# One block of float32 products per chunk, regrouped tiles in halves, and regrouping issued in three parts

## The chip, the core and the metric

The kernel runs on one core of a Trainium2 chip. Its engines are TensorE (PE; its weight loads stand apart as PEld), VectorE (DVE), ScalarE (ACT), GpSimd (POOL) and SyncE (SP), which here issues the DMAs. The metric is the device time of one execution in microseconds, the median of several runs.

## The reference

Three stages follow each other. Cut to what is computed:

```python
X = np.fft.rfft(x, axis=1)                       # x: 8 x 3072 x 256
Y = soft_threshold(X @ (w_r + i w_i) + b, 0.01)  # real and imaginary part apart
x = np.fft.irfft(Y, n=3072, axis=1).reshape(24576, 256)
h = x @ moe_w_in                                 # 256 -> 2048
x = (h - np.tanh(h)) @ moe_w_out                 # 2048 -> 256
logits = x @ phi                                 # 32 slots
d = softmax(logits, axis=0);  slot_in = d.T @ x
slot_out = experts(slot_in)                      # 8 experts, 4 slots each, relu between w1 and w2
out = softmax(logits, axis=1) @ slot_out
```

## The kernel before

The Fourier stage writes its result to DRAM; the token stage reads it back in 48 chunks of 512 tokens; the expert stage runs last. What the change touches is the token stage, and its loop over chunks is most of the time.

A chunk c is loaded transposed as y (128 x 1024). The product with `moe_w_in` is made by a seven-product scheme on 2 x 2 blocks: `wino(c, w, n)`, called P, is six TensorE instructions of 128 x 256 in float32r (a value split into a high and a low part), for one of four column groups w and one of seven products n. A call with n = 1, 4, 6 or 7 is followed by a ScalarE copy of its PSUM bank (line 797). The calls 1, 6, 7 and 4 of one w add to the same bank, so each waits until the copy before it has read the bank. `add` (A, line 804, VectorE) adds a second bank; `gate` (G, line 808, ScalarE) applies tanh. There are eight g tiles per chunk, p = 0 to 7, and six PSUM banks in rotation for P.

The g tiles are used three times, each with plain float32 products of 32 output columns, four of which (a = 0 to 3) lie side by side in the array:

- L, `logit_mm(c, p)`, line 927: the logits, for two g tiles a call, p = 0, 2, 4, 6; the last call adds the four products of line 935 on the raw y tile `yr`.
- DY, `dy_mm(c)`, line 846, and D, `dg_mm(c)`, line 1057: the slot sums, softmax weights `et` times the g values. They want tokens on the partitions. So VectorE transposes each g tile in 32 x 32 blocks (T, `turn_g`, line 878; `turn_yr`, TD, line 867) into two staging tiles, gt0 (g tiles 0 to 3 and yr) and gt1 (4 to 7), with one buffer each, and 32 DMAs per chunk put the blocks into place (`regroup`, "reg", line 894): 16 of 160 KB from gt0, 16 of 128 KB from gt1. Their targets are the four `gq` tiles of a chunk, 9 KB per partition each, out of a ring of five. D makes 16 instructions of 128 x 512 from them; each counts as two in the profile, as every float32 product does.
- `accum_y` and `accum` (accy, acc) then add the PSUM results to running sums.

The order of all engines inside a chunk is written out by hand in the tuple `PLAN`: an entry is a step, its chunk relative to the current one (-1 the one before) and its arguments. Each engine runs its instructions in that order. Before, L of the last three g pairs, ("L", -1, 2) to ("L", -1, 6), stands early in the pass of the next chunk; ("L", 0, 0), ("DY", -1), ("D", -1) stand near the end of the pass.

All DMAs of the token stage are issued by SP, in program order. They share eight semaphores in turn, so a DMA isn't issued before the one eight places earlier has landed. Per chunk SP issues y, yr, the store of the combine weights (line 1041), then reg(-1, 1), then reg(0, 0). In the last chunk the entries ("W", ...) issue expert weights between them.

Of the kernel before, what the change touches and what calls it, by code (L numbers as in the profile page):

```python
# [28 lines left out]
PLAN = (  # L29
# [10 lines left out]
)  # L40
# [608 lines left out]
def token_phase(tc, nch, yd, wh, wl, wp, wy, ident, ew):  # L649
# [9 lines left out]
    with ExitStack() as ctx:  # L659
# [80 lines left out]

        homes = chain(["g5"] + [f"g{k}" for k in range(5)], cycle([f"g{k}" for k in range(5)] + [f"x{k}" for k in range(4)]))

        def g_tile(c, p):
            k = next(homes)
            g = gs[c, p] = (ew.gtp if k == "g5" else ew.gp if k[0] == "g" else ew.txp).tile(
                [128, 2, 512], F32, tag=k, name="g", bufs=1
            )
            return g
# [86 lines left out]
        def dy_mm(c):  # L835


            beside = c < nch - 1
            o = dy[c] = lp[c + 1][:, 256:320] if beside else bank()[:, 0:64]
            if beside:  # L840
                y = [g[:, 0:256].rearrange("p (k f) -> p k f", k=4) for g in gq[c]]
            else:
                y = [yq[c][:, a] for a in range(4)]
            for k in range(4):
                for a in (3, 2, 1, 0):
                    nc.tensor.matmul(
                        o[32 * a:32 * a + 32], ex[c][:, k, :], y[a][:, k], start=k == 0 and not beside, stop=k == 3,
                        skip_group_check=True,
                    )
# [35 lines left out]

        def regroup(c, h):

            t = gt.pop((c, h))
            if h == 0:
                gq[c] = [ew.gq_tile([128, 2304]) for _ in range(4)]  # L890
            for a in range(4):
                o = gq[c][a][:, 1280 * h:1280 + 1024 * h]
                for q in range(4):
                    nc.sync.dma_start(out=o[32 * q:32 * q + 32], in_=t[32 * a:32 * a + 32, q])  # L894

# [74 lines left out]
        def soft_max(c):  # L970
            o = lr[c]
            m = sp.tile([64, 1], F32, tag="m", name="m", bufs=1)
            m2 = sp.tile([32, 1], F32, tag="m2", name="m2", bufs=1)
# [71 lines left out]
        def dg_mm(c):  # L1045

            o = dp[c] = ps2.tile([128, 512], F32, tag="d", name="pd")
            if c < nch - 1:
                parts = [(
                    slice(0, 512), [g[:, 256:2304].rearrange("p (h k f) -> p k h f", h=2, k=4) for g in gq.pop(c)],  # L1050
                )]
            else:
                parts = [(slice(256 * h, 256 * h + 256), [gl[h][:, :, a] for a in range(4)]) for h in range(2)]
# [40 lines left out]
        def chunk(c):  # L1094

            for name, d, *args in PLAN:
# [8 lines left out]
                elif k > 0 and k < nch or k == 0 and name not in "PAG":  # L1105
                    if k < nch - 1 or name not in ("T", "TD", "reg"):
                        if c < nch - 1 or name not in ("D", "DY", "accy"):
                            do(name, k, *args)

        def weights(w):  # L1110

            if w == 0:
                ew.load(12, "y")
                ew.load_ct(0, 16)
            elif w == 1:
                do("reg", nch - 2, 1)
                ew.load_m()
# [12 lines left out]
        for s in range(8):  # L1130
# [30 lines left out]
            if s == 6:  # L1161
                sum_w(1, nc.vector, ((ew.txp, "x2"), (ew.txp, "x3")))
                split_sw(1)
                do("TD", c)
                do("reg", c, 0)
                sum_w(2, nc.vector, ((ew.txp, "x0"), (ew.txp, "x1")))
                sum_w(3, nc.gpsimd, ((ew.txp, "x2"), (ew.gqp, "gq4")))
            yield
# [62 lines left out]
class ExpertWeights:  # L1231
# [6 lines left out]
    def __init__(self, tc, ctx, nch, w1, w2, w_out, md, ctd):  # L1238
# [5 lines left out]
        self.cts = {}  # L1244
        self.turn = 0
        self.spare = {}
# [15 lines left out]
    def open_late(self):  # L1262

        self.tyq = self.pool("tx2", 1)
        pool = self.pool("tc", 1, side="right")
        pool.tile([128, 48], F32, name="pad")
        self.acc = pool.tile([128, 512], F32, name="acc")
# [12 lines left out]

    def gq_tile(self, shape, dtype=F32, k=None):
        if k is None:
            k = self.turn
            self.turn += 1
        return self.gqp.tile(shape, dtype, tag=f"gq{k % 5}", name="gq")

    def load_wo(self):
        w = self.w_out.rearrange("(p F) m -> p F m", F=16)
        self.wo = []
        self.wt = [self.gq_tile([128, 8, 256]) for _ in range(2)]  # L1290
        for k in range(4):
            u = self.wt[k // 2][:, 4 * (k % 2):4 * (k % 2) + 4]
            self.tc.nc.sync.dma_start(out=u, in_=w[:, 4 * k:4 * k + 4])
            self.wo.append(u)

    def load_ct(self, c0, c1):
        n = c1 - c0
        u = self.gtp.tile([128, n, 128], F32, tag="gt1", name="ect", bufs=1) if c0 else self.gq_tile([128, n, 128])
        for c in range(c0, c1, 16):
            m = min(c + 16, c1)  # L1300
            self.tc.nc.sync.dma_start(out=u[:, c - c0:m - c0], in_=self.ctd[:, c:m])
        for c in range(c0, c1, 8):
            self.cts[c] = u[:, c - c0:c - c0 + 8]

# [4 lines left out]
    def pieces(self, j, home):  # L1309
# [18 lines left out]
        if home == "gq":  # L1328
            t = self.gq_tile([128, 2048])
            return [t[:, 512 * i:512 * i + 512] for i in range(4)]  # L1330
        return [u for i in range(2) for u in tile(self.txp, f"x{(2 * j + i) % 4}")]
# [17 lines left out]
def expert_phase(tc, nch, ew, ident, out):  # L1349

    nc = tc.nc
    with ExitStack() as ctx:
# [71 lines left out]
        for i in range(0, nch, 2):  # L1424
# [84 lines left out]
```

## Time and profile before

| | us |
|---|---|
| median of three runs (2195.88 to 2200.4) | 2196.58 |
| the profiled execution, its own time | 2199.71 |
| its span in the trace | 2197.9 |
| PE busy (96% of the span) | 2113.1 |
| DVE busy (83%) | 1825.5 |
| ACT busy (63%) | 1392.0 |
| POOL busy (29%) | 637.3 |

The trace is one execution. An engine's busy time is the union of its instructions; matmul ends are modelled. A wait is put down to what released it. "x32" merges neighbours with the same line. The time from the start of one D (line 1057) to that of the next is the time of a chunk.

### The profile page before, as it was taken

To read this page: it belongs to the slowest core of one execution; us is meant where nothing else is said; L and a number is where in the kernel's file an instruction comes from. 1 tells how busy PE (TensorE), PEld (TensorE's weight loads), DVE (VectorE), ACT (ScalarE), POOL (GpSimd) and SP (SyncE) were. 2 spreads that over 40 slices of the span, in tenths; PEclk is the share of its full clock that TensorE was granted. 3 is DMA by queue.
4 is the path that set the end of the run, shared out by engine and by line. 5 is a ranking of instruction groups with operands and counts; after the bars stand their busy time and mean duration, and the time that the engine had idled before them with its cause. 6 is when DMAs were issued, how large, how long until landed. Compare 5 with 4: busy or idle time off the path is not lost.

```text
span 2197.9 us, 50700 instructions
## 1 busy us (share of the span) xinstructions
PE 2113.1 (96%) x19546; PEld 1755.6 (80%) x19546; DVE 1825.5 (83%) x3650; ACT 1392.0 (63%) x2309; POOL 637.3 (29%) x655
## 2 busy tenths in 40 slices
PE   7999999999999999999999999999999999999976
PEld 3678888888888888888888888888888888888743
DVE  4999989988995888888888888888888888888634
ACT  3466666666655666666676676666667676666623
POOL 1433334434442422222222222222222222222100
PEclk8999999999999999999999999999999999999995
DMA  9678888889666888888888888888888888888899
GB/s 287 207 228 263 249 264 279 249 252 281 193 199 193 200 213 200 206 201 199 202 202 202 205 207 212 200 209 196 196 205 203 199 203 211 202 209 203 239 366 391
DMA packets 251951, 495.76 MB, mean 226 GB/s; under 512 B 36160, under 2 KB 144960, under 8 KB 251328
## 3 DMA queue, kind: packets, MB, share of 16 engines
q1 hardware_dynamic: 251600, 492.49, 82.8%
q8 instruction: 155, 2.54, 0.5%
q14 instruction: 84, 0.69, 0.1%
q10 hardware_dynamic: 112, 0.04, 0.0%
HBM read 164.45 MB, written 106.17 MB: 123 GB/s over the span
## 4 chain that ended last, share of the span: by engine, by line
PE 68%; DMA 14%; SPq 11%; DVE 4%; issue 2%; ACT 1%; POOL 0%; ACTq 0%; POOLq 0%; DVEq 0%
PE ph L786 25%; SPq L894 10%; PE pd L1057 8%; DMA yr<-yd 6%; PE pmix L321 6%; PE pl L927 5%; PE pf L247 5%; PE pi L406 5%; PE pf L280 3%; DMA gq<-gt 3%; PE pi L378 3%; PE pa L321 3%; DMA ewt<-in_moe_w 1%; PE ph L757 1%; DMA out_dram<-ot 1%
## 5 line engine op out<-in xcount | busy, mean ns | idle before, releaser
L797 ACT ACTIVATE g<-ph 128x512 f32<-128x512 f32 x752 | 440.4, 592 | 347.4 <-PE ph L786 326.8
L878 DVE STREAM_TRANSPOSE gt<-g 128x512 f32<-128x512 f32 x752 | 482.4, 684 | 39.5 <-ACT g L808 32.5
L786 PE MATMUL ph<-th,s 128*128 128x256 f32 x2256 | 477.3, 284 | 5.5 <-ACT g L797 4.5
L804 DVE TENSOR_TENSOR g<-ph,g 128x512 f32<-128x512 f32 x564 | 366.4, 676 | 128.8 <-PE ph L786 96.4
L786 PEld LDWEIGHTS ph<-th,s 128*128 128x128 f32 x2256 | 378.1, 190 | 25.5 <-issue 18.9
L808 ACT ACTIVATE g<-g 128x1024 f32<-128x1024 f32 x376 | 390.3, 1052 | 1.8 <-DVE g L804 0.3
L786 PE MATMUL ph<-tl,s 128*128 128x256 f32 x1128 | 318.4, 282 | 0.0
L786 PE MATMUL ph<-yh,wl 128*128 128x256 f32 x1128 | 316.3, 280 | 0.0
L786 PE MATMUL ph<-y,wh 128*128 128x256 f32 x1128 | 315.9, 280 | 0.0
L786 PE MATMUL ph<-yh,wh 128*128 128x256 f32 x1128 | 315.4, 280 | 0.0
L699 POOL TENSOR_TENSOR tl<-tr,th 128x512 fp32r<-128x512 f32 x94 | 121.5, 1293 | 595.9 <-ACT th L698 590.6
L371 POOL TENSOR_TENSOR sw<-t,c 64x256 f32<-64x256 f32 x192 | 169.5, 883 | 157.0 <-DVE c L363 131.7
L786 PEld LDWEIGHTS ph<-tl,s 128*128 128x128 f32 x1128 | 214.0, 190 | 0.0
L786 PEld LDWEIGHTS ph<-yh,wh 128*128 128x128 f32 x1128 | 213.6, 189 | 0.0
L786 PEld LDWEIGHTS ph<-y,wh 128*128 128x128 f32 x1128 | 212.7, 189 | 0.0
L786 PEld LDWEIGHTS ph<-yh,wl 128*128 128x128 f32 x1128 | 212.5, 188 | 0.0
L1057 PE MATMUL pd<-gq,et 128*32 128x512 f32 x1504 | 181.8, 593 | 17.8 <-DMA gq<-gt 16.6
L927 PE MATMUL pl<-g,wp 128*32 128x256 f32 x3072 | 185.9, 382 | 0.0
L693 POOL TENSOR_TENSOR tr<-y 128x256 f32<-128x256 f32 x92 | 68.1, 740 | 401.5 <-DMA y<-yd 401.5
L406 PEld LDWEIGHTS pi<-i,v 96*128 96x128 f32 x1024 | 127.5, 191 | 26.2 <-issue 20.8
L1057 PEld LDWEIGHTS pd<-gq,et 128*32 128x32 f32 x1504 | 86.6, 109 | 75.6 <-issue 22.6
L247 PE MATMUL pf<-xt,c 96*96 96x512 f32 x256 | 134.1, 618 | 11.4 <-DMA xt<-in_x 6.6
(217 smaller groups left out, 4387.3 us busy)
## 6 DMA issues: line engine op xcount, KB each, us to landing
gq<-gt SPq DMA_DIRECT2D x752, 160.0 KB, 3.4
gq<-gt SPq DMA_DIRECT2D x752, 128.0 KB, 3.5
xt<-in_x SPq DMA_DIRECT2D x64, 384.0 KB, 5.3
vd<-vs SPq DMA_DIRECT2D x96, 256.0 KB, 3.2
v<-vd SPq DMA_DIRECT2D x64, 384.0 KB, 5.2
yd<-yt SPq DMA_DIRECT2D x48, 512.0 KB, 5.5
y<-yd SPq DMA_DIRECT2D x48, 512.0 KB, 5.2
yr<-yd SPq DMA_DIRECT2D x48, 512.0 KB, 7.0
```

The costliest lines, as they stand in the source:

```text
L247: nc.tensor.matmul(p[:96], c1, x[:, s], start=True, stop=True)
L321: nc.tensor.matmul(o, st[u], w[m], start=first and k == 0, stop=last and k == 2)
L371: eng.tensor_tensor(out=v[64 * ri:64 * ri + 64, gg], in0=t[q, e], in1=c[q, e], op=ALU.subtract)
L406: nc.tensor.matmul(p[:, a, :], t[:, 4 * u + a, :], i2[:, 96 * n2:96 * n2 + 128], start=True, stop=True)
L786: nc.tensor.matmul(o[:, 256 * j:256 * j + 256], a[u][:, 128 * j:128 * j + 128], y[v], start=new and j == 0 and k == 0, stop=n in (2, 3, 4) ...
L797: nc.scalar.activation(e[n], o.rearrange("p (j n) -> p j n", j=2), AF.Copy)
L804: nc.vector.tensor_tensor(out=h, in0=o, in1=h, op=ALU.add)
L808: nc.scalar.activation(g, g, AF.Tanh)
L878: nc.vector.transpose(out=t[:, :, :, 2 * (p % 4) + u, :], in_=g[:, u, :].rearrange("p (q k i) -> p q k i", q=4, k=4))
L894: nc.sync.dma_start(out=o[32 * q:32 * q + 32], in_=t[32 * a:32 * a + 32, q])
L927: nc.tensor.matmul(lp[c][q:q + 32, 0:256], wp[:, 2 * p + f, :], half_of(c, gs[c, p + f // 2][:, f % 2], h), start=p == 0 and f < 2, stop=F ...
L1057: nc.tensor.matmul(o[32 * a:32 * a + 32, f], ex[c][:, k, :], g[a][:, k], start=k == 0, stop=k == 3)
```

## The change

The entries of `PLAN` are put in another order. In it ("L", -1, 0), ("DY", -2), ("L", -1, 2), ("D", -2), ("L", -1, 4) and ("L", -1, 6) follow each other: the slot sums of a chunk are made two passes after it, in the same place as the logits of the chunk between. `regroup` has three parts: 0 and 1 move two of the four a-blocks of gt0 each, 2 moves all of gt1. The `gq` tiles become halves, six of 5 KB (tags h0 to h5, from gt0) and four of 4 KB (q0 to q3, from gt1), and D makes two runs of 16 instructions of 128 x 256, one from each half. The ring of g tiles has one more (x5). Loads of the expert stage that used the old ring use the new ones.

```diff
 PLAN = (
-    ("S", 0, 2), ("loady", 1), ("T", -1, 4), ("T", -1, 7), ("G", -1, 6), ("W", 0, 0), ("P", 0, 0, 6), ("L", -1, 2), ("L", -1, 4),
...
+    ("G", -1, 6), ("P", 0, 0, 6), ("A", 0, 0, 2), ("T", -1, 7), ("loady", 1), ("splity", 1), ("L", -1, 0), ("DY", -2), ("L", -1, 2),
+    ("D", -2), ("L", -1, 4), ("L", -1, 6), ("P", 0, 0, 7), ("P", 0, 1, 1), ("sum", -1), ("P", 0, 1, 2), ("P", 0, 0, 4), ("P", 0, 1, 6),
...
-        homes = chain(["g5"] + [f"g{k}" for k in range(5)], cycle([f"g{k}" for k in range(5)] + [f"x{k}" for k in range(4)]))
+        homes = chain(["g5"] + [f"g{k}" for k in range(5)], cycle([f"g{k}" for k in range(5)] + [f"x{k}" for k in range(4)] + ["x5"]))
...
-                y = [g[:, 0:256].rearrange("p (k f) -> p k f", k=4) for g in gq[c]]
+                y = [g[:, 0:256].rearrange("p (k f) -> p k f", k=4) for g in gq[c, 0]]
...
-        def regroup(c, h):
-
-            t = gt.pop((c, h))
-            if h == 0:
-                gq[c] = [ew.gq_tile([128, 2304]) for _ in range(4)]
-            for a in range(4):
-                o = gq[c][a][:, 1280 * h:1280 + 1024 * h]
+        def regroup(c, part):
+
+            h = part // 2
+            t = gt[c, h]
+            o = gq.setdefault((c, h), [])
+            for a in ((0, 1), (2, 3), (0, 1, 2, 3))[part]:
+                o.append(ew.gq_tile([128, 1280 - 256 * h], h))
                 for q in range(4):
-                    nc.sync.dma_start(out=o[32 * q:32 * q + 32], in_=t[32 * a:32 * a + 32, q])
+                    nc.sync.dma_start(out=o[a][32 * q:32 * q + 32], in_=t[32 * a:32 * a + 32, q])
+            if part:
+                del gt[c, h]
...
             if c < nch - 1:
-                parts = [(
-                    slice(0, 512), [g[:, 256:2304].rearrange("p (h k f) -> p k h f", h=2, k=4) for g in gq.pop(c)],
-                )]
+                parts = [(
+                    slice(256 * h, 256 * h + 256),
+                    [g[:, 256 - 256 * h:].rearrange("p (k f) -> p k f", k=4) for g in gq.pop((c, h))],
+                ) for h in range(2)]
...
-                        if c < nch - 1 or name not in ("D", "DY", "accy"):
-                            do(name, k, *args)
+                        do(name, k, *args)
...
-    def gq_tile(self, shape, dtype=F32, k=None):
-        if k is None:
-            k = self.turn
-            self.turn += 1
-        return self.gqp.tile(shape, dtype, tag=f"gq{k % 5}", name="gq")
+    def gq_tile(self, shape, h=0):
+        k = self.turn[h]
+        self.turn[h] += 1
+        return self.gqp.tile(shape, F32, tag=f"q{k % 4}" if h else f"h{k % 6}", name="gq")
```

TensorE around D, before (pl are logits and DY, pd is D, ph are the products P):

```order
L786 MATMUL ph<-tl,s 128x256
L786 MATMUL ph<-th,s 128x256
L927 MATMUL pl<-g,wp 32x256 x8
L846 MATMUL pl<-gq,et 32x64 x16
L1057 MATMUL pd<-gq,et 32x512 x16
L786 MATMUL ph<-th,wh 128x256
...
L786 MATMUL ph<-tl,s 128x256
L786 MATMUL ph<-th,s 128x256
L927 MATMUL pl<-g,wp 32x256 x24
L935 MATMUL pl<-yr,wy 32x256 x4
L786 MATMUL ph<-th,s 128x256
```

The same place now, lines shifted by up to four:

```order
L787 MATMUL ph<-th,s 128x256
L930 MATMUL pl<-g,wp 32x256 x8
L847 MATMUL pl<-gq,et 32x64 x16
L930 MATMUL pl<-g,wp 32x256 x8
L1061 MATMUL pd<-gq,et 32x256 x32
L930 MATMUL pl<-g,wp 32x256 x16
L938 MATMUL pl<-yr,wy 32x256 x4
L787 MATMUL ph<-th,s 128x256
```

Two blocks of float32 products per chunk have become one, and D is 32 instructions of 256 columns in place of 16 of 512.

SP, one chunk before (y and yr are loads, ctd the store of combine weights, gq the regrouping):

```order
L673 DMA y<-yd_68 128x1024
L815 DMA yr<-yd_68 128x1024
L1041 DMA ctd<-le 128x128
L894 DMA gq<-gt 32x1024 x16
L894 DMA gq<-gt 32x1280 x16
```

And now:

```order
L674 DMA y<-yd_67 128x1024
L895 DMA gq<-gt 32x1280 x16
L1044 DMA ctd<-le 128x128
L816 DMA yr<-yd_67 128x1024
L895 DMA gq<-gt 32x1024 x16
```

The 16 DMAs from gt1, which were in the middle of SP's round, now end it; y follows behind them, and yr stands just ahead of them.

VectorE from `accum` to the transposes of gt1, before (et is the softmax weights, gt<-g are transposes, 4x4x32 into gt0 and 16x32 into gt1):

```order
L1065 SCALAR_TENSOR_TENSOR acc<-acc,al,pd 128x512
L804 TENSOR_TENSOR g<-ph,g 128x2x256
L960 TENSOR_TENSOR le<-pl,le 64x256
L804 TENSOR_TENSOR g<-ph,g 128x2x256
...
L878 STREAM_TRANSPOSE gt<-g 128x4x4x32 x2
L804 TENSOR_TENSOR g<-ph,g 128x2x256 x2
L867 STREAM_TRANSPOSE gt<-yr 128x4x4x32 x2
L804 TENSOR_TENSOR g<-ph,g 128x2x256 x2
L878 STREAM_TRANSPOSE gt<-g 128x4x4x32 x4
```

And now:

```order
L805 TENSOR_TENSOR g<-ph,g 128x2x256 x2
L1069 SCALAR_TENSOR_TENSOR acc<-acc,al,pd 128x512
L1006 STREAM_TRANSPOSE et<-le 64x128 x2
L1010 TENSOR_SCALAR ssum<-ssum,al,rs 64x1
L1013 COPY al<-al 64x1
L879 STREAM_TRANSPOSE gt<-g 128x4x4x32 x2
L805 TENSOR_TENSOR g<-ph,g 128x2x256 x4
L868 STREAM_TRANSPOSE gt<-yr 128x4x4x32 x2
L879 STREAM_TRANSPOSE gt<-g 128x4x4x32 x6
L879 STREAM_TRANSPOSE gt<-g 128x16x32 x2
L805 TENSOR_TENSOR g<-ph,g 128x2x256
```

`accum` and the transposes of et now stand in the middle of the chunk ahead of a run of four adds, and the transposes into gt0 stand together near its end, followed by the first into gt1.

## Rows read from the trace of the kernel before

**Rows 1.** Busy time of each engine in 40 chunks, from one D's start to another's
```profile
core 0: us, PE busy (x) PEld busy (x) DVE busy (x) ACT busy (x) POOL busy (x), PEclk, DMA share, GB/s
825.40:1984.70 1159.30, 1144.25 (x12172) 979.20 (x12161) 1002.72 (x2041) 796.88 (x1281) 311.66 (x281) 1.00 0.84 203
```

**Rows 2.** Timeline of PE at two neighbouring D: start us, us, what, count
```profile
1172.99 0.83 PE L1057 MATMUL pd<-gq,et 128*32 128x512 f32 x4
...
1201.44 0.83 PE L1057 MATMUL pd<-gq,et 128*32 128x512 f32 x4
```

**Rows 3.** Timeline of PE, a block with D that waits for a regrouping DMA
```profile
1431.75 0.63 PE L846 MATMUL pl<-gq,et 128*32 128x64 f32 x32
1433.40 3.87 PE L1057 MATMUL pd<-gq,et 128*32 128x512 f32 x32 [1.02 <-DMA gq<-gt]
```

**Rows 4.** Groups of PE instructions in these 40 chunks: busy, mean ns, idle before
```profile
L1057 PE MATMUL pd<-gq,et 128*32 128x512 f32 x1280 | 154.7, 593 | 14.6 <-DMA gq<-gt 13.4 <-issue 1.1
```

**Rows 5.** Timeline of PE, both float32 blocks of a chunk and their edges
```profile
1402.55 0.63 PE L846 MATMUL pl<-gq,et 128*32 128x64 f32 x32
1403.03 3.87 PE L1057 MATMUL pd<-gq,et 128*32 128x512 f32 x32
1406.83 0.38 PE L786 MATMUL ph<-th,wh 128*128 128x256 f32 x1
...
1410.92 0.28 PE L786 MATMUL ph<-tl,s 128*128 128x256 f32 x1
1411.04 0.28 PE L786 MATMUL ph<-th,s 128*128 128x256 f32 x1
1411.25 2.80 PE L927 MATMUL pl<-g,wp 128*32 128x256 f32 x48
1413.87 0.61 PE L935 MATMUL pl<-yr,wy 128*32 128x256 f32 x8
1414.41 0.39 PE L786 MATMUL ph<-th,s 128*128 128x256 f32 x1
1414.63 0.28 PE L786 MATMUL ph<-tl,s 128*128 128x256 f32 x1
```

**Rows 6.** Timeline of PE, the last chunk's D, in 64 products of 256 columns
```profile
2092.04 3.66 PE L1057 MATMUL pd<-gl,et 128*32 128x256 f32 x64
```

**Rows 7.** Timeline: end of one call P on PE, then its copy on ACT
```profile
1407.52 0.28 PE L786 MATMUL ph<-th,wl 128*128 128x256 f32 x1
...
1407.83 0.60 ACT L797 ACTIVATE g<-ph 128x512 f32<-128x512 f32 x1 [3.81 <-PE ph L786]
```

**Rows 8.** Timeline of DVE: transposes, et, a run of four adds
```profile
1401.38 0.63 DVE L1003 STREAM_TRANSPOSE et<-le 64x128 f32<-64x128 f32 x2
...
1402.48 1.30 DVE L878 STREAM_TRANSPOSE gt<-g 128x512 f32<-128x512 f32 x2
1403.71 0.58 DVE L1021 STREAM_TRANSPOSE lt<-le 64x128 f32<-64x128 f32 x2
...
1405.74 2.47 DVE L804 TENSOR_TENSOR g<-ph,g 128x512 f32<-128x512 f32 x4
1408.14 0.27 DVE L854 SCALAR_TENSOR_TENSOR accy<-accy,al,pl 128x64 f32<-128x64 f32 x1
```

**Rows 9.** Group of DVE in the 40 chunks
```profile
L1065 DVE SCALAR_TENSOR_TENSOR acc<-acc,al,pd 128x512 f32<-128x512 f32 x40 | 28.2, 705 | 0.0
```

**Rows 10.** Timeline of SP: one chunk's DMA issues
```profile
1386.63 1.22 SPq L673 DMA_DIRECT2D y<-yd  x1
1387.95 0.39 SPq L815 DMA_DIRECT2D yr<-yd  x1
1388.44 0.37 SPq L1041 DMA_DIRECT2D ctd<-le  x1
1388.87 26.66 SPq L894 DMA_DIRECT2D gq<-gt  x32
1415.64 0.67 SPq L673 DMA_DIRECT2D y<-yd  x1
```

**Rows 11.** Waits of SP in the 40 chunks: total us, times, longest
```profile
SPq L894 <- DVE lt L1021: 114.6, 40, 4.6
SPq L894 <- DMA yr<-yd: 67.3, 40, 3.3
SPq L894 <- PE pd L1057: 37.5, 36, 2.3
SPq L894 <- DMA y<-yd: 8.9, 17, 1.7
```

**Rows 12.** DMA issues of the page: size, median us from issue to landing
```profile
gq<-gt SPq DMA_DIRECT2D x752, 128.0 KB, 3.5
...
y<-yd SPq DMA_DIRECT2D x48, 512.0 KB, 5.2
yr<-yd SPq DMA_DIRECT2D x48, 512.0 KB, 7.0
```

More of the change, by code (lines that the diff above doesn't have):

```diff
@@ L738, in bank @@
             return (ps if k < 4 else ps2).tile([128, 512], F32, tag=f"b{k}", name="ph")
-        homes = chain(["g5"] + [f"g{k}" for k in range(5)], cycle([f"g{k}" for k in range(5)] + [f"x{k}" for k in range(4)]))
+        homes = chain(["g5"] + [f"g{k}" for k in range(5)], cycle([f"g{k}" for k in range(5)] + [f"x{k}" for k in range(4)] + ["x5"]))
         def g_tile(c, p):
             k = next(homes)
-            g = gs[c, p] = (ew.gtp if k == "g5" else ew.gp if k[0] == "g" else ew.txp).tile(
+            g = gs[c, p] = (ew.gtp if k == "g5" else ew.gp if k[0] == "g" else ew.tyq if k == "x5" else ew.txp).tile(
                 [128, 2, 512], F32, tag=k, name="g", bufs=1
@@ L971, in soft_max @@
             o = lr[c]
-            m = sp.tile([64, 1], F32, tag="m", name="m", bufs=1)
+            m = ew.tcp.tile([64, 1], F32, tag="m", name="m")
             m2 = sp.tile([32, 1], F32, tag="m2", name="m2", bufs=1)
@@ L1113, in weights @@
                 ew.load(12, "y")
+            elif w == 1:
+                for part in range(3):
+                    do("reg", nch - 2, part)
                 ew.load_ct(0, 16)
-            elif w == 1:
-                do("reg", nch - 2, 1)
                 ew.load_m()
@@ L1165, in token_phase @@
                 do("reg", c, 0)
+                do("reg", c, 1)
                 sum_w(2, nc.vector, ((ew.txp, "x0"), (ew.txp, "x1")))
-                sum_w(3, nc.gpsimd, ((ew.txp, "x2"), (ew.gqp, "gq4")))
+                sum_w(3, nc.gpsimd, ((ew.txp, "x2"), (ew.gqp, "h5")))
             yield
@@ L1178, in token_phase @@
             do("G", c, 2 * w + 1)
+        do("L", c, 0)
         do("DY", c - 1)
@@ L1244, in __init__ @@
         self.cts = {}
-        self.turn = 0
+        self.turn = [0, 0]
         self.spare = {}
@@ L1264, in open_late @@
         self.tyq = self.pool("tx2", 1)
-        pool = self.pool("tc", 1, side="right")
-        pool.tile([128, 48], F32, name="pad")
+        pool = self.tcp = self.pool("tc", 1, side="right")
+        pool.tile([128, 40], F32, name="pad")
+        pool.tile([64, 1], F32, tag="m", name="m")
         self.acc = pool.tile([128, 512], F32, name="acc")
@@ L1289, in load_wo @@
         self.wo = []
-        self.wt = [self.gq_tile([128, 8, 256]) for _ in range(2)]
         for k in range(4):
-            u = self.wt[k // 2][:, 4 * (k % 2):4 * (k % 2) + 4]
+            u = self.gq_tile([128, 4, 256])
             self.tc.nc.sync.dma_start(out=u, in_=w[:, 4 * k:4 * k + 4])
@@ L1296, in load_ct @@
     def load_ct(self, c0, c1):
[L1297 to L1303, printed above, removed]
+        if c0:
+            n = c1 - c0
+            u = self.gtp.tile([128, n, 128], F32, tag="gt1", name="ect", bufs=1)
+            for c in range(c0, c1, 16):
+                m = min(c + 16, c1)
+                self.tc.nc.sync.dma_start(out=u[:, c - c0:m - c0], in_=self.ctd[:, c:m])
+            for c in range(c0, c1, 8):
+                self.cts[c] = u[:, c - c0:c - c0 + 8]
+        else:
+            for c in range(c0, c1, 8):
+                self.cts[c] = self.gq_tile([128, 8, 128])
+                self.tc.nc.sync.dma_start(out=self.cts[c], in_=self.ctd[:, c:c + 8])
     def load_m(self):
@@ L1328, in pieces @@
         if home == "gq":
-            t = self.gq_tile([128, 2048])
-            return [t[:, 512 * i:512 * i + 512] for i in range(4)]
+            t = [self.gq_tile([128, 1024], 1) for _ in range(2)]
+            return [u[:, 512 * i:512 * i + 512] for u in t for i in range(2)]
         return [u for i in range(2) for u in tile(self.txp, f"x{(2 * j + i) % 4}")]
@@ L1433, in expert_phase @@
                 if home < 4:
-                    ot = ew.gq_tile([128, 4, 256], k=ew.turn + 1 + home)
+                    ot = ew.gq_tile([128, 4, 256], 1)
                 else:
```

18 rows, old and new, of the table PLAN are left out of this document.

## Prediction

> **What bounds the kernel now.** I read the page first: PE is busy 96% of the span, the next engine 83%. Then the engines in a stretch of 40 whole chunks [rows 1]: PE 1144.3 of 1159.3 us at full granted clock, DVE 1002.7, ACT 796.9, DMA share 0.84. A chunk takes 1159.3 / 40 = 28.98 us and PE is idle for little of it, so the token stage is bound by what PE is given to do, and by the few waits inside that. Next the D starts, chunk by chunk: two neighbours are 28.45 us apart [rows 2], among the shortest of the stage; the mean is 0.53 us longer. The reader should see in [rows 3] where that goes: DY starts at 1431.75 and D at 1433.40, 1.65 us later, with a wait for a regrouping DMA; where nothing waits the same step takes 0.48 us [rows 5]. Last I read DVE, ACT and SP for what stands close behind PE: DVE has (1159.3 - 1002.7) / 40 = 3.9 us free per chunk, and SP waits about 5.7 us per chunk in all [rows 11], 2.9 of it for transposes (named L1021, the instruction that starts as the transpose ends).
>
> **The change part by part.**
>
> *One float32 block instead of two.* The edges of a block cost PE time. Entering: the last P product starts at 1411.04 and the first L at 1411.25, 0.21 us against 0.12 between P products, so 0.09. Leaving: 48 products of L run from 1411.25 to 1413.87 in 12 sets of four, 0.218 us a set; the two sets of line 935 should end at 1414.31, and P starts at 1414.41, 0.10 late; the product after it comes 0.22 later instead of 0.12, again 0.10 [rows 5]. Together 0.29 us. All steps inside the new block are float32 to float32, and the old block already has two of these (L to DY, DY to D) without such an edge. Removed in 46 chunks: 46 x 0.29 = 13.3 us.
>
> *D in halves.* D runs from 1403.03 to the next P at 1406.83, 3.80 us, of which 0.10 is the leaving edge: 3.70 [rows 5]. Now it is 16 sets of four 256-column products; at L's pace that is 16 x 0.218 = 3.49. The same form stands in the trace once, in the last chunk: 3.66 us for all 64, with the last product's full run in it [rows 6]. So D gains between 0.04 and 0.21 us. I take 0.21, since the set pace excludes the drain that the next products cover: 47 x 0.21 = 9.9 us.
>
> *The wait of D.* Before, gt1 is regrouped in the same pass that D reads it. Now D reads the tiles one pass after, and its first half reads those from gt0, which were moved first. From SP's round: the last DMAs of gt1 are issued about 10.6 us (below) after the last transpose into gt1 and land 3.5 us later [rows 12], which puts them about 2 us into the next pass; D's second half starts about 4.7 us into it (P 0.7, L 0.9, DY 0.5, L 0.9, half of D 1.7). So the wait goes, with over 2 us to spare. Its size lies between 0.37 us a chunk, PE's own idle time before D, 14.6 / 40 [rows 4], and the 0.53 between the mean and the short chunk. I take 0.45: 46 x 0.45 = 20.7 us.
>
> *What the new order adds on PE.* P(0, 2, 6) now has a single call between it and P(0, 2, 1), whose copy it waits for. The last product of a call starts at 1407.52; its copy starts at 1407.83 and takes 0.60, so ends 0.91 us after [rows 7]. A call with one call between would start 7 x 0.118 = 0.83 after. That is 0.08 plus the signalling, which the row does not show; I take 0.12: 46 x 0.12 = 5.5 us. The other copies have two calls or more between and are covered.
>
> *What it moves.* On DVE acc, et and one transpose now stand ahead of four adds, and P(1, 0, 5) takes the bank that the last of them frees. From the copy after P(0, 2, 7): copy 0.64, two adds 1.2, acc 0.70, et 1.10, transpose 1.23, four adds 2.40 = 7.3 us [rows 7, 8, 9]. PE has 11 calls in between, 11 x 0.71 = 7.8. It holds by 0.5 us. If that cover is gone, every 0.1 us costs 4.6. ACT's gates pile up behind the last P calls of a pass; the float32 block, about 8 us in which PE needs no copy, lets them drain. splity now stands in this place and needs y, which SP issues after the 16 DMAs of gt1: see the rivals. POOL's order of work is the same. The extra g tile only relaxes a reuse. For jitter in all this, none to 0.2 us a chunk; I take 0.1: 4.6 us. At the ends one D moves from before the last pass into it and the expert loads keep their volume: nothing, give or take 3 us.
>
> *Sum.* 13.3 + 9.9 + 20.7 - 5.5 - 4.6 = 33.8 us. From the profiled execution's own time, 2199.71, that is 2165.9. The execution is 3.1 above the median of the runs, 2196.58, so I forecast about 2162 for a median.
>
> **The rivals.**
>
> *The regrouping wait moves to DVE.* There is one gt1, so the first transpose into it at the end of a pass, T(0, 5), needs the 16 DMAs landed. SP has 35 DMAs in a round [rows 10] and issues one per (28.98 - 5.7) / 35 = 0.665 us, so 16 take 10.6, and landing 3.5: 14.1 us after the last transpose of the old content. DVE has between the two: 7 adds 4.2, combine 2.0, accy 0.3, acc 0.7, et 1.1, five transposes 6.2 = 14.5 us [rows 8, 9, 12]. For it: the margin is 0.4 us plus DVE's own waits, and yr, 7.0 us from issue to landing, holds up the DMA eight places on, as it does now (67.3 us in 40 chunks, 1.7 each) [rows 11, 12]. Against it: PE notices only through the gate of the tile that the next add completes, which is needed in the last L, about 1 us after it should be there. A lateness of 1.7 less these 1.4 is 0.3 us, with jitter 0.4 a chunk: 46 x 0.4 = 18, 2180.
>
> *DVE becomes the bound on PE's banks.* If the 7.3 us are 8.2, PE waits 0.4 in each chunk. For it: the chain starts behind the combine steps, which wait themselves. Against: 3.9 us of idle DVE in a chunk. 2180 too.
>
> *The halves gain nothing.* If the second half's own waits at its first products spread the four column positions apart, as in D before, D stays at 3.70: 2162 + 10 = 2172. The Trainium skill, TensorE: Matmul & The Clock Gate, section Back-to-back issue gap, adds a fixed 2.5 ns to each warm product whatever its width, which speaks against more and narrower products; by it D would become an estimated 0.04 us longer and the time about 2174. No row shows that cost; the set pace above says shorter.
>
> *The saving is eaten whole.* Bank, gate and regrouping waits add up to about 0.7 us a chunk: 2194, no change.
>
> *Slower: y comes too late.* ACT does its work in order, and splity stands ahead of the copy after P(0, 0, 7), on which P(0, 0, 4) waits. y is issued after the 16 DMAs of gt1, about 2 us before the pass begins, and lands 5.2 us after issue [rows 12], about 3 into it; ACT comes to splity at about 6 to 7. Past 8 us into the pass each microsecond of lateness is one of PE: 46 us. It has to be late by 5 us beyond its median to start, and by 6 for 2162 + 46 = 2208. For it: SP's round is full for 23 of 29 us, and each hold-up ahead of y adds. Against: SP's 2.9 us wait for transposes is free to take up delays.
>
> **How the numbers follow.** Forecast, 2162: 0.57. Regrouping wait at 2180: 0.13. DVE bound at 2180: 0.09. Halves at 2172: 0.06. Eaten whole at 2194: 0.07. Slower at 2208: 0.08. A measurement of this kernel can tell about 0.2%, 4.4 us: the first four are faster, 0.85; same 0.07; slower 0.08. The low end takes the upper bounds and no new wait: 13.3 + 9.9 + 24.4 = 47.6, 2149. The high end takes in the rivals at 2180 with the 0.1 us of their sizes' doubt (4.6) and 3 for the ends: 2187. That leaves out about 0.15 above and a little below.
>
> **What would show it.** Right: D starts about 28.2 us apart; one entry and one exit edge per chunk; 16 sets of D at 0.22; no wait of line 1061 for a DMA; a short wait, near 0.1, at P(0, 2, 6) for ACT. Wrong: DVE transposes into gt1 that wait for DMAs gq<-gt by over 1 us, with PE waiting for ACT's gates at the last L; PE waiting for adds at P(1, 0, 5); ACT's splity waiting for y; or D starts 28.8 us apart or more. The forecast fails if any of these holds in most chunks.

## The result and the profile after

The changed kernel takes 2175.32 us (median of four runs, 2173.43 to 2177.67), the kernel before, measured beside it, 2198.49 us (2195.88 to 2201.02). The ratio is 0.9895, with a 95% interval of 0.9878 to 0.9913: faster by 23 us. The forecast was 2162, the range 2149 to 2187. The time lies inside, 13 us above the forecast, so a third of the expected gain of 34 us is missing. The profiled execution took 2174.94 us and its span is 2173.1.

The first view answers to [rows 1], with its columns: busy time of each engine over 40 whole chunks of the kernel after.

```profile
837.00:1965.20 1128.20, 1128.07 (x13444) 988.81 (x13440) 1041.29 (x2041) 814.76 (x1281) 313.86 (x280) 1.00 0.87 209
```

A chunk now takes 1128.2 / 40 = 28.21 us, where it took 28.98, and PE is busy for 1128.1 of 1128.2 us. The timeline of PE shows one chunk's float32 block with its edges, and the D of the chunks ahead and behind (start us, duration us, what, count); it answers to [rows 2, 5].

```profile
977.95 3.64 PE L1061 MATMUL pd<-gq,et 128*32 128x256 f32 x64
...
1003.75 0.28 PE L787 MATMUL ph<-th,s 128*128 128x256 f32 x1
1003.96 1.07 PE L930 MATMUL pl<-g,wp 128*32 128x256 f32 x16
...
1006.15 3.64 PE L1061 MATMUL pd<-gq,et 128*32 128x256 f32 x64
1009.61 1.91 PE L930 MATMUL pl<-g,wp 128*32 128x256 f32 x32
1011.33 0.61 PE L938 MATMUL pl<-yr,wy 128*32 128x256 f32 x8
1011.88 0.38 PE L787 MATMUL ph<-th,s 128*128 128x256 f32 x1
1012.10 0.28 PE L787 MATMUL ph<-tl,s 128*128 128x256 f32 x1
...
1034.53 3.64 PE L1061 MATMUL pd<-gq,et 128*32 128x256 f32 x64
```

D follows D after 28.20 us here (977.95 to 1006.15). Of the 45 intervals between the first and the 46th D, 44 are 28.20 to 28.22 us, and one is 28.38 (the next one in these rows, with a wait for an add of VectorE at P(0, 2, 5)). Before, they ranged from 28.45 to 30.4. No step inside the block waits, and D's wait for the regrouping DMAs, 13.4 us in 40 chunks [rows 4], is gone, as the group of D over the same 40 chunks shows (busy, mean ns, idle before).

```profile
L1061 PE MATMUL pd<-gq,et 128*32 128x256 f32 x2560 | 145.5, 379 | 0.0
```

**Where the missing gain is.** The starts of D divide the span into three parts: up to the first D, 45 chunks, and from the 46th D to the end. The kernels of the experiments below are in the table too; "usual" is the median interval.

| kernel | first D | 45 intervals: mean, usual | 46th D to the end | span |
|---|---|---|---|---|
| before | 738.8 | 28.97, 28.87 | 155.4 | 2197.9 |
| after | 752.3 | 28.21, 28.20 | 151.5 | 2173.1 |
| y of chunk 2 split later | 748.2 | 28.21, 28.20 | 152.2 | 2169.6 |
| y of chunk 2 issued earlier | 740.1 | 28.21, 28.21 | 152.9 | 2162.6 |
| two float32 blocks again | 752.7 | 28.68, 28.65 | 152.9 | 2196.1 |
| before, with D in halves | 741.2 | 28.36, 28.25 | 154.9 | 2172.1 |
| order with P(0, 1, 4) between | 750.2 | 28.79, 28.79 | 151.7 | 2197.4 |
| earlier y, order with P(0, 1, 7) between | 742.2 | 28.04, 27.99 | 151.3 | 2155.2 |

The chunks bring 1303.7 - 1269.3 = 34.4 us, against 33.8 in the forecast's sum. D stands elsewhere in the pass, so a shift at one end comes back at the other; together the two ends lose 13.5 - 3.9 = 9.6 us, where the forecast had nothing, give or take 3. The first part holds the Fourier stage too, which none of the edits touches, and the traces differ there by up to 4 us: the first product of the token stage starts at 665.62 before and at 665.93 after. The loss lies in the first pass that goes by the table. The same 20 us of both kernels, first before, then after:

```profile
720.00:740.00 20.00, 19.49 (x186) 18.39 (x189) 14.27 (x31) 15.27 (x24) 8.58 (x10) 0.90 0.75 192
```

```profile
720.00:740.00 20.00, 10.35 (x70) 9.95 (x71) 8.93 (x18) 8.86 (x17) 8.62 (x8) 0.74 0.51 131
```

PE works 10.4 us instead of 19.5. The timelines of SP, of ACT and of PE of the kernel after say why (what ended an idle time stands in brackets):

```profile
710.00 11.41 SPq L895 DMA_DIRECT2D gq<-gt  x16
721.51 0.70 SPq L674 DMA_DIRECT2D y<-yd  x1
```

```profile
726.52 1.06 ACT L679 ACTIVATE yh<-y 128x1024 fp32r<-128x1024 f32 x1 [14.13 <-DMA y<-yd]
727.49 1.06 ACT L798 ACTIVATE g<-ph 128x512 f32<-128x512 f32 x2
```

```profile
728.12 0.58 PE L787 MATMUL ph<-th,wh 128*128 128x256 f32 x1 [11.75 <-ACT g L798]
728.50 0.41 PE L787 MATMUL ph<-tl,wh 128*128 128x256 f32 x1
728.71 0.41 PE L787 MATMUL ph<-th,wl 128*128 128x256 f32 x1
```

Read from the bottom: PE waits 11.75 us for a copy on ACT. That copy stands behind the split of y of chunk 2 (line 679), which waits 14.13 us for its DMA. That DMA is issued only at 721.51, behind the 16 regrouping DMAs of chunk 0, and lands 5.0 us later. In the kernel before it is issued at 721.37, just as late, but there the split stands in the middle of the pass, and ACT comes to it at 730.16 without a wait for it. The timelines of SP and of ACT of the kernel before:

```profile
721.37 0.69 SPq L673 DMA_DIRECT2D y<-yd  x1
```

```profile
730.16 1.05 ACT L678 ACTIVATE yh<-y 128x1024 fp32r<-128x1024 f32 x1
```

After the idle time the clock costs a little more: the rows of PE above show products 0.21 us apart instead of 0.12, and the next view the granted clock at 0.50 (1.2 GHz) from 728 to 730 and back at 1.00 (2.4 GHz) from 732 (stretch, its length, busy time by engine as in [rows 1], clock, DMA share, GB/s).

```profile
716.20:728.00 11.80, 0.16 (x2) 0.00 (x0) 4.39 (x7) 1.48 (x3) 3.96 (x6) 0.71 0.85 222
728.00:730.00 2.00, 1.89 (x9) 1.89 (x10) 1.82 (x4) 1.00 (x4) 1.47 (x3) 0.50 0.00 0
...
732.00:734.00 2.00, 2.00 (x20) 2.00 (x19) 1.24 (x3) 2.00 (x4) 0.57 (x1) 1.00 0.00 0
```

One more thing in the steady chunks differs from the forecast: P(0, 2, 6) costs more than was put down. In the timeline of PE, from two neighbouring windows of time, the first row is the last product of P(0, 2, 5), the second the first of P(0, 2, 6) and the third its second.

```profile
990.73 0.28 PE L787 MATMUL ph<-th,s 128*128 128x256 f32 x1
990.99 0.39 PE L787 MATMUL ph<-th,s 128*128 128x256 f32 x1
991.21 0.28 PE L787 MATMUL ph<-tl,s 128*128 128x256 f32 x1
```

The step to the first product is 0.26 us here (0.256 in the median of the chunks), against 0.12 between products that follow each other; its weight load waits for the copy on ACT, which ends at 990.94. The step from the first to the second is 0.22 us, late as well. So the call is late by 0.138 + 0.105 = 0.24 us a chunk.

The last pass has a stall of its own, which no experiment touches. Of PE's waits behind 1990 us, 2.8 us are D's for the regrouping (2.1 before), and 5.5 us are one for `yr` of the last chunk, which the kernel before doesn't have:

```profile
2059.76 1.94 PE L828 MATMUL ph<-ident,yr 128*128 128x128 f32 x8 [5.52 <-DMA yr<-yd]
```

SP issues this `yr` at 2052.55, behind 16 regrouping DMAs and loads for the expert stage. What the stall is worth is not shown; the part from the 46th D to the end is 3.9 us shorter than before all the same.

### The profile page after: what moved, and what is told of

It reads as the page before. It is cut to its first block, busy times and chain, and to the rows that moved or that the text cites. A ratio compares the mean times of both kernels' runs of the same rounds, so it can differ in the third digit from the quotient of the medians.

```text
span 2173.1 us, 53805 instructions
## 1 busy us (share of the span) xinstructions
PE 2091.0 (96%) x21050; PEld 1765.8 (81%) x21050; DVE 1869.7 (86%) x3650; ACT 1412.0 (65%) x2309; POOL 639.9 (29%) x655
## 4 chain that ended last, share of the span: by engine, by line
PE 88%; DVE 5%; DMA 3%; ACT 1%; issue 1%; SPq 1%; POOL 0%; ACTq 0%; DVEq 0%; POOLq 0%
PE ph L787 43%; PE pl L930 8%; PE pd L1061 7%; PE pmix L322 6%; PE pi L407 5%; PE pf L248 5%; PE pf L281 3%; PE pi L379 3%; PE pa L322 3%; SPq L895 1%; PE pl L847 1%; PE pl L938 1%; PE ph L758 1%; DVE sw L372 1%; PE p_out L1367 1%
## 5 line engine op out<-in xcount | busy, mean ns | idle before, releaser
L798 ACT ACTIVATE g<-ph 128x512 f32<-128x512 f32 x752 | 447.5, 596 | 320.3 <-PE ph L787 284.2
L787 PE MATMUL ph<-th,s 128*128 128x256 f32 x2256 | 499.1, 288 | 1.8 <-POOL s L731 0.9
L879 DVE STREAM_TRANSPOSE gt<-g 128x512 f32<-128x512 f32 x752 | 472.2, 679 | 6.0 <-ACT g L761 4.6
L809 ACT ACTIVATE g<-g 128x1024 f32<-128x1024 f32 x376 | 380.5, 1050 | 47.4 <-DVE g L805 47.4
L787 PEld LDWEIGHTS ph<-th,s 128*128 128x128 f32 x2256 | 383.6, 189 | 30.6 <-issue 19.3
L930 PE MATMUL pl<-g,wp 128*32 128x256 f32 x3072 | 193.7, 381 | 0.0
L1061 PE MATMUL pd<-gq,et 128*32 128x256 f32 x3008 | 171.3, 379 | 2.8 <-DMA gq<-gt 2.8
L1061 PEld LDWEIGHTS pd<-gq,et 128*32 128x32 f32 x3008 | 98.0, 110 | 67.3 <-issue 3.3
L414 ACT ACTIVATE yt<-pi 128x384 f32<-128x384 f32 (+1 forms) x128 | 114.3, 894 | 46.1 <-PE pi L407 45.6
```

The source lines that it names most:

```text
L787: nc.tensor.matmul(o[:, 256 * j:256 * j + 256], a[u][:, 128 * j:128 * j + 128], y[v], start=new and j == 0 and k == 0, stop=n in (2, 3, 4) ...
L798: nc.scalar.activation(e[n], o.rearrange("p (j n) -> p j n", j=2), AF.Copy)
L809: nc.scalar.activation(g, g, AF.Tanh)
L879: nc.vector.transpose(out=t[:, :, :, 2 * (p % 4) + u, :], in_=g[:, u, :].rearrange("p (q k i) -> p q k i", q=4, k=4))
L930: nc.tensor.matmul(lp[c][q:q + 32, 0:256], wp[:, 2 * p + f, :], half_of(c, gs[c, p + f // 2][:, f % 2], h), start=p == 0 and f < 2, stop=F ...
L1061: nc.tensor.matmul(o[32 * a:32 * a + 32, f], ex[c][:, k, :], g[a][:, k], start=k == 0, stop=k == 3)
```

## Experiments

Three theories had to be told apart. The first: the missing gain is the wait for y in the first pass, and the steady chunks behave as forecast. The second: the halves of D do nothing, and order and lag do it all. The third: the new order has merely put new waits, of banks and copies, in the place of old ones. Ratios are to runs of the kernel before that were made beside each group of experiments: their median was 2197.88 for the first four, 2199.07 for the next two and 2196.50 for the last.

**The split of y one place later.** In the pass of chunk 1 alone, the split of y of chunk 2 goes to where the low part is made.

```diff
+                if c == 1 and name == "splity":
+                    continue
+                if c == 1 and name == "lowy":
+                    do("splity", k)
```

> The changed kernel, but in the first pass that loads a chunk (c = 1) ScalarE's splity stands just ahead of low_y, a quarter of a pass later, and not ahead of the copies. Theory (the change lost about 12 us there, because ScalarE, in order, stood 14.1 us behind y of chunk 2): the 14.1 us wait goes, the first pass is about 11 us shorter, 2164 us against 2175. Rival (the first pass is slow because of GpSimd's sums and splits of the weights and the lower clock, and the wait for y is only what shows): the time goes to another wait in that pass, 2173 to 2176.

Measured: 2171.40 us, ratio 0.9878 (0.9852 to 0.9903). By its number alone this run does not decide: 2171 lies nearer to the rival's 2173 than to the theory's 2164. The steady chunks are unchanged, and the first D comes 4 us earlier, not 11; 1 us of the 4 is from the Fourier stage (token stage from 664.96). PE's waits between 700 and 760 us were 13.2 us in the kernel after; here they are these (total, times, longest):

```profile
PE ph L787 <- POOL s L731: 6.0, 1, 6.0
PE ph L787 <- ACT g L798: 2.6, 1, 2.6
```

ACT no longer holds PE up for long, but GpSimd does: it too does its work in order, and four instructions on y (line 694) stand ahead of the splits of weights for which PE now waits. Its timeline:

```profile
725.72 0.72 POOL L694 TENSOR_TENSOR tr<-y 128x256 f32<-128x256 f32 x1 [7.75 <-DMA y<-yd]
...
728.57 1.80 POOL L731 TENSOR_TENSOR s<-sw,s 128x768 fp32r<-128x768 f32 x1
```

So the place of the split was only part of it; the late y blocks two engines. The size expected here was wrong; the next run tests the cause (y) by itself.

**y of chunk 2 ahead of the regrouping of chunk 0.** Nothing else is moved; the three new lines replace the two "reg" lines further down.

```diff
             if s == 7:
+                do("loady", 2)
+                do("reg", c, 0)
+                do("reg", c, 1)
...
                 do("TD", c)
-                do("reg", c, 0)
-                do("reg", c, 1)
```

> The changed kernel, but y of chunk 2 is issued ahead of the 16 regrouping DMAs of chunk 0 and not behind them. Theory (what is late is the issue of y, 11.4 us of regrouping ahead of it on SP): y is issued near 711 and lands near 717, ScalarE's wait shrinks from 14.1 to about 4 us, 2166 us. Rival (GpSimd's weight sums hold the first pass): 2173 to 2176. A second rival (regrouping of chunk 0, now later, is missed by someone): over 2177.

Measured: 2165.66 us (2164.47 to 2167.14), ratio 0.9852 (0.9822 to 0.9882). SP issues y at 707.37, ACT splits it at 710.90, and the waits of PE between 700 and 760 us fall to 4.2 us, below the 5.0 of the kernel before:

```profile
PE ph L787 <- ACT g L798: 3.2, 2, 2.6
PE ph L787 <- DVE g L805: 0.7, 1, 0.7
PE ph L787 <- POOL s L731: 0.3, 1, 0.3
```

The first D comes at 740.1 instead of 752.3; the token stage began 2.1 us earlier in this trace (663.85), so about 10 of these 12 us are the edit's, and the medians too differ by 10. The two ends together gain 1.2 us against the kernel before (+1.3 and -2.5; a loss of 0.6 without the earlier beginning) where the kernel after loses 9.6. This is the missing gain, but for 2 to 4 us.

**Two float32 blocks again.** L of p = 4 and 6 goes behind two P calls; the lag of D and the halves stay.

```diff
-    ("D", -2), ("L", -1, 4), ("L", -1, 6), ("P", 0, 0, 7), ("P", 0, 1, 1), ("sum", -1), ("P", 0, 1, 2), ("P", 0, 0, 4), ("P", 0, 1, 6),
+    ("D", -2), ("P", 0, 0, 7), ("P", 0, 1, 1), ("L", -1, 4), ("L", -1, 6), ("sum", -1), ("P", 0, 1, 2), ("P", 0, 0, 4), ("P", 0, 1, 6),
```

> The changed kernel, but two calls P stand between D and the last two L calls, so that a chunk has two blocks of float32 products again. Theory (each block costs 0.29 us in its entry and exit): chunks of 28.20 + 0.29 = 28.49 us, 46 x 0.29 = 13.3, 2188 us. Rival (the edges cost nothing by themselves and the gain was D's wait and the halves alone): 28.2 us, 2175.

Measured: 2195.46 us (2191.43 to 2199.10), ratio 0.9988 (0.9975 to 1.0002). The usual chunk is 28.65 us, longer by 0.45 instead of the expected 0.29. The edges at which the block is cut, in the timelines of PE and of ACT:

```profile
1039.74 3.64 PE L1061 MATMUL pd<-gq,et 128*32 128x256 f32 x64
1043.40 0.39 PE L787 MATMUL ph<-th,s 128*128 128x256 f32 x1
1043.63 0.28 PE L787 MATMUL ph<-tl,s 128*128 128x256 f32 x1
...
1044.79 0.28 PE L787 MATMUL ph<-yh,wl 128*128 128x256 f32 x1
1045.00 1.93 PE L930 MATMUL pl<-g,wp 128*32 128x256 f32 x32
```

```profile
1041.81 1.06 ACT L809 ACTIVATE g<-g 128x1024 f32<-128x1024 f32 x1 [1.00 <-DVE g L805]
1042.77 0.58 ACT L798 ACTIVATE g<-ph 128x512 f32<-128x512 f32 x1
```

From D's start to the next P it is 3.66 us, 0.20 more than to the next L in the kernel after (1006.15 to 1009.61). The second P product is 0.11 late, and the entry into the second block (0.21 instead of 0.12) costs 0.09. That makes 0.40 of the 0.45. Half of the 0.20 is a wait of its own (without it the step takes 3.57 us, as the next experiment shows): P(0, 0, 7) starts at 1043.40, as the copy after P(0, 0, 6) ends at 1043.35, which stands on ACT behind a gate that waits for VectorE. In the kernel after, the rest of the block lies over this copy. So one block is worth some 0.3 us of edges and, in this order, 0.1 of cover for that copy. The last 0.05 is not placed.

**The kernel before with D in halves, and nothing else.**

```diff
-                    slice(0, 512), [g[:, 256:2304].rearrange("p (h k f) -> p k h f", h=2, k=4) for g in gq.pop(c)],
-                )]
+                    slice(256 * h, 256 * h + 256),
+                    [g[:, 256 + 1024 * h:1280 + 1024 * h].rearrange("p (k f) -> p k f", k=4) for g in gq[c]],
+                ) for h in range(2)]
+                del gq[c]
```

> The kernel before, but D in two runs of 256 columns, the first from the half of the gq tiles that came from gt0. Nothing else. Theory of the prediction (D shorter by 0.21 us, and its wait of about 0.45 us is one for the second half's tiles, which the first half now covers with 1.7 us): D's run 3.5 us, no wait of 1 us left, chunks near 28.3, 2198 - 9.9 - 20.7 = 2168 us. Rival 1 (the halves gain only their pace, the wait stays as the regrouping falls behind with the rest): 2188. Rival 2 (nothing gained, a fixed cost for each product): 2198 or more.

Measured: 2172.96 us (2165.92 to 2173.92), ratio 0.9876 (0.9846 to 0.9905): by itself as much as the whole change. Two things happen. The undisturbed chunk falls from 28.45 [rows 2] to 28.25 us:

```profile
1083.60 3.64 PE L1059 MATMUL pd<-gq,et 128*32 128x256 f32 x64
1087.17 0.38 PE L786 MATMUL ph<-th,wh 128*128 128x256 f32 x1
1087.39 0.28 PE L786 MATMUL ph<-tl,wh 128*128 128x256 f32 x1
...
1111.85 3.64 PE L1059 MATMUL pd<-gq,et 128*32 128x256 f32 x64
```

D and its leaving edge take 3.57 us where they took 3.80 [rows 5]. The start of the last product of D and the next P are 0.31 us apart, against 0.52 before: the saving sits at the end of D, where the last product is half as long. And the wait for the regrouping nearly goes, though D still reads tiles that were regrouped in the same pass: the mean over 45 chunks lies 0.11 us above the usual chunk, where the mean before lay 0.52 above 28.45. Between 840 and 1950 us PE's waits are these:

```profile
PE ph L786 <- DVE g L804: 1.0, 2, 0.7
PE pd L1059 <- DMA gq<-gt: 0.5, 1, 0.5
PE pd L1059 <- issue: 0.4, 1, 0.4
```

The likely reason, not shown by itself: D's first half needs only the part that was moved first, and its second half starts 1.7 us later than D as a whole did.

**Two calls between P(0, 2, 1) and P(0, 2, 6).** P(0, 1, 4) goes between, and P(0, 3, 1) up ahead of P(0, 2, 7), so that this one doesn't come too close to P(0, 2, 6) in turn.

```diff
-    ("P", 0, 2, 1), ("P", 0, 2, 5), ("P", 0, 2, 6), ("S", 0, 3), ("exp", -1), ("P", 0, 1, 4), ("P", 0, 1, 3), ("P", 0, 2, 7), ("W", 0, 1),
-    ("P", 0, 3, 1), ("P", 0, 3, 5), ("P", 0, 3, 2), ("comb", -1), ("accy", -2), ("A", 0, 2, 7), ("A", 0, 1, 3), ("G", 0, 0),
+    ("P", 0, 2, 1), ("P", 0, 2, 5), ("P", 0, 1, 4), ("S", 0, 3), ("exp", -1), ("P", 0, 2, 6), ("P", 0, 1, 3), ("P", 0, 3, 1), ("P", 0, 2, 7),
+    ("W", 0, 1), ("P", 0, 3, 5), ("P", 0, 3, 2), ("comb", -1), ("accy", -2), ("A", 0, 2, 7), ("A", 0, 1, 3), ("G", 0, 0),
```

> The changed kernel with one alteration of its order: two plain calls now stand between P(0,2,1) and P(0,2,6) (P(0,2,5) and P(0,1,4)) instead of one, and P(0,3,1) moves up ahead of P(0,2,7). Theory: in the changed kernel P(0,2,6) begins 0.138 us late and its second product another 0.105 us late in every chunk, because ScalarE's copy after P(0,2,1) has ended only then; with two calls between it has ended long before, so a chunk falls from 28.20 to about 27.96 us and the kernel by 0.24 x 46 = 11 us, from 2175 to about 2164. Rival: ScalarE or VectorE is late for whichever call comes there, so that a wait of the same size stands at P(0,1,4), at P(0,2,6) or at the next call that writes over a copied bank, the chunk stays at 28.2 us and the kernel at 2175. The loss in the first pass (the wait for y of chunk 2) is left as it is in both.

Measured: 2200.65 us, ratio 1.0014 (1.0000 to 1.0027), a loss of 25 us against the kernel after. The rival was right in kind and too mild: the chunk became 28.79 us. The wait at P(0, 2, 6) is gone, and three others stand in its place, each with a late second product behind it: P(0, 2, 7), 0.15 + 0.105 us; P(0, 3, 3), 0.05 + 0.10; P(1, 0, 5), 0.38 + 0.105, where the kernel after had 0.08 in all. That is 0.90 for 0.32, the 0.58 that the chunk grew by. ACT's timeline shows the first cause: the softmax's exp and two small instructions behind it, until 1053.4, now stand ahead of the copy after P(0, 2, 6), and the copies behind it are late.

```profile
1052.49 0.51 ACT L994 ACTIVATE le<-le,nm 64x256 f32<-64x256 f32 x1
...
1053.30 1.27 ACT L798 ACTIVATE g<-ph 128x512 f32<-128x512 f32 x2
1054.94 0.60 ACT L798 ACTIVATE g<-ph 128x512 f32<-128x512 f32 x1 [0.37 <-PE ph L787]
```

The last of these is the copy after P(0, 2, 7), one call later in the pass than before. With it starts the chain on VectorE that ends with four adds, and P(1, 0, 5) waits for the last of them (VectorE, then PE):

```profile
1059.84 2.44 DVE L805 TENSOR_TENSOR g<-ph,g 128x512 f32<-128x512 f32 x4
```

```profile
1061.84 0.28 PE L787 MATMUL ph<-yh,wl 128*128 128x256 f32 x1
1062.34 0.39 PE L787 MATMUL ph<-th,s 128*128 128x256 f32 x1 [0.23 <-DVE g L805]
```

From 1054.94 to the end of the adds, 1062.28, it is 7.34 us. The prediction had worked this chain out as 7.3 us.

**The same order with the earlier y.**

> The changed kernel with both repairs: y of chunk 2 is issued ahead of the regrouping of chunk 0, and two calls stand between P(0,2,1) and P(0,2,6). Theory: the two losses lie in different places (the first pass, and once in every chunk) and add up: 2166 us, as measured with the earlier y alone, less 0.24 x 46 = 11 us gives about 2155, with chunks of about 27.96 us and no wait of TensorE over 5 us in the first pass. Rival: the wait in the steady chunks moves on instead of going, so that this kernel takes the 2166 us of the earlier y alone and its chunks stay at 28.2 us.

Measured: 2190.91 us (2188.56 to 2194.49), ratio 0.9966 (0.9951 to 0.9980), with the same 28.79 us a chunk. The earlier y brings its 10 us here too; the order costs its 25.

**P(0, 2, 1) and P(0, 1, 7) change places, with the earlier y.** The copy in question comes one call sooner, and all behind P(0, 2, 6) stays where it is.

```diff
-    ("S", 0, 2), ("lowy", 1), ("P", 0, 1, 5), ("P", 0, 0, 3), ("P", 0, 1, 7), ("max", -1), ("A", 0, 0, 3), ("T", -1, 6), ("A", 0, 1, 7),
-    ("P", 0, 2, 1), ("P", 0, 2, 5), ("P", 0, 2, 6), ("S", 0, 3), ("exp", -1), ("P", 0, 1, 4), ("P", 0, 1, 3), ("P", 0, 2, 7), ("W", 0, 1),
+    ("S", 0, 2), ("lowy", 1), ("P", 0, 1, 5), ("P", 0, 0, 3), ("P", 0, 2, 1), ("max", -1), ("A", 0, 0, 3), ("T", -1, 6), ("P", 0, 1, 7),
+    ("A", 0, 1, 7), ("P", 0, 2, 5), ("P", 0, 2, 6), ("S", 0, 3), ("exp", -1), ("P", 0, 1, 4), ("P", 0, 1, 3), ("P", 0, 2, 7), ("W", 0, 1),
```

> The kernel with the earlier y of chunk 2, and in its order only P(0,2,1) and P(0,1,7) change places, so that P(0,1,7) and P(0,2,5) stand between P(0,2,1) and P(0,2,6); nothing behind P(0,2,6) moves, unlike in the run in which P(0,3,1) was moved up too. Theory: the wait of 0.138 + 0.105 us at P(0,2,6) goes, nothing takes its place, since ScalarE's and VectorE's work at the end of the pass keeps its place, and chunks fall from 28.21 to about 27.97 us: 2166 - 11 = 2155 us. Rival: ScalarE's copies stand one call closer to their banks' next use wherever a call is moved up, so that waits of at least the same sum stand at later calls (as at P(0,2,7), P(1,0,5) and P(1,0,2) in that run), and the kernel takes 2166 us or more.

Measured: 2157.76 us (2156.63 to 2163.85), ratio 0.9825 (0.9803 to 0.9847), the fastest of all: better than both kernels. D starts follow each other like this:

```profile
1051.43 3.64 PE L1061 MATMUL pd<-gq,et 128*32 128x256 f32 x64
...
1079.41 3.64 PE L1061 MATMUL pd<-gq,et 128*32 128x256 f32 x64
```

The usual chunk is 27.98 us, 0.22 shorter, so the 0.24 us at P(0, 2, 6) were on the path and nothing took their place. The mean is 28.04, as four of 45 intervals are 0.4 to 1.0 us longer, each with a wait at P(0, 2, 5) for an add of VectorE. With them the 45 intervals bring about 8 us, and not 10 or 11: the span is 7.4 us below that of the kernel with the earlier y, the median 7.9.

## Why the prediction was right, and where it was off

Point by point, in its own steps:

- **One float32 block, 0.29 us.** Right in size for the edges. The kernel before with D in halves, whose two blocks don't wait for ACT, shows 0.09 for the entry, 0.11 for leaving D, 0.105 for the second product behind it: 0.31. Without these, and with 0.24 added for P(0, 2, 6) and 0.08 for P(1, 0, 5) (last section), its 28.25 becomes 28.26; measured 28.20. So by the chunks the block is worth up to 0.37.
- **D in halves, 0.21 us.** Right: 28.45 to 28.25, 0.20. The pace of the sets was the right row to price it by: from D to the next L it is 3.46 us in the kernel after, 16 sets at 0.216. The Trainium skill, TensorE: Matmul & The Clock Gate, section Back-to-back issue gap, adds 2.5 ns to each warm product, by which D would have become longer; no such lengthening shows, D with its edge became 0.23 us shorter with twice the products.
- **The wait of D, 0.45 us.** It went, and its size was 0.52, by the mean and the undisturbed chunk. The prediction put the lag of a pass first and the order of the halves beside it. The halves alone remove 0.41 of it, and on top of them the lag adds at most 0.11. The change without the halves was not run, so what the lag would remove by itself stays open.
- **P(0, 2, 6), -0.12 us.** The place was right, the size was half: 0.24. The working counted only the copy that ends late. A product that starts late makes the next one late too, here by 0.105; the prediction had seen this at the block's exit [rows 5] and not carried it over. This term was mis-sized by 0.12 x 45 = 5.4 us.
- **Jitter, -0.1 us.** There is none: 44 of 45 intervals agree within 0.02 us. This gives back 4.5 us, so that with the larger wait of D the chunks came out as forecast, 34.4 us against 33.8. Part of that agreement is luck: these two cancel what P(0, 2, 6) costs above its price and the 0.08 us at P(1, 0, 5), which had none.
- **VectorE's chain, margin 0.5 us.** Its length was nearly right: 7.3; 7.46 us in the kernel after, from the start of the copy after P(0, 2, 7), 1022.50, to the end of the last add. The cover of 11 calls, 7.8 us, was counted from the start of the first of them, 1022.30, though the copy starts 0.20 us later; from there it is 7.55. In the kernel after the margin is 0.1 us, as the timelines of VectorE and of PE show: the adds end at 1027.40 + 2.56 = 1029.96, and P(1, 0, 5) starts at 1030.05. Of that, little is free: in the order that moved P(0, 2, 7) back by a call, P(1, 0, 5) does wait, and starts 0.06 us after its last add ends (1062.28, 1062.34). That order shows what a lost cover costs there. VectorE as a bound was thus close, but it did not come true.

```profile
1027.40 2.56 DVE L805 TENSOR_TENSOR g<-ph,g 128x512 f32<-128x512 f32 x4
```

```profile
1030.05 0.36 PE L787 MATMUL ph<-th,s 128*128 128x256 f32 x1
```

- **The regrouping wait on VectorE.** It did not come: between 840 and 1950 us VectorE waits 0.5 us for a DMA, once, and by the trace it is that of y.
- **y comes too late.** In the steady chunks it does not; ACT's split waits for no DMA there, and y lands 3.5 us after issue (5.2 before [rows 12]). The mechanism came true once, in the first pass, and that is **the step that failed: "At the ends ... nothing, give or take 3 us"**. The ends lost 9.6 us, and putting y of chunk 2 ahead of the regrouping of chunk 0 brought about 10 back. The rival was worked out for the table's own rhythm, in which y was to be issued about 2 us before the pass begins (in the steady pass shown above it is at 1003.27, 0.7 us ahead of the first L). In the pass that starts the rhythm it is issued 10 us into it (721.51, the pass's first L at 711.69), behind DMAs that stand in code outside the table, whose place ahead of y the change left alone while it moved y's first reader forward.

With that one repair the kernel takes 2165.66 us, beside the 2162 of the forecast. That the time lay in the range without it is luck as well: the high end, 2187, was set by rivals at 2180 that did not come true, and their room took up a loss at the ends three times as large as was allowed for.

## What to carry to other kernels

When a table of work is moved about, the passes that fill and drain it need their own check: for the first reader of each tile, what is queued ahead of its load on the issuing engine, and which engines, in order, stand behind that reader. An added stall on TensorE costs its own length and about 0.1 us more here for the product behind it, and what it takes to remove one depends on what every other engine has queued behind the call that is moved: two ways to do it gave +25 us and about -8 us. A regrouping that is consumed in the order in which it is moved, half by half, can hide most of its wait without another pass of lag.

## What the runs showed of the hardware

The late second product is the unexpected part. Whether the first product of a P call is late by 0.05, 0.14, 0.15 or 0.38 us, or comes behind a float32 block, the second follows it after 0.22 us instead of 0.12 (0.104 to 0.105 more in each of these places). A late product itself shows 0.38 or 0.39 us in the profile instead of 0.28. One place differs, P(1, 0, 5) in the kernel after, with 0.08 more behind a first product that is on time. The runs don't say what this is; they only show that many short stalls cost more than the waits that a view of waits lists.

Behind a single idle stretch of 11.75 us TensorE's granted clock was low for up to 4 us more: 0.50 (1.2 GHz) from 728 to 730 us, with products 0.21 us apart, 0.63 in the mean of the next 2 us, and 1.00 from 732. In the kernel with the earlier y, whose longest wait of PE between 700 and 760 us is 2.6 us, it is 1.00 in the same stretch, 716.2 to 732 us.
